# A decode kernel of two layers, its order of work and its transfers planned anew: 83 half tiles kept in place of 80

## The chip, the cores and the metric

One core of a Trainium2 chip runs the whole program in one launch. The metric is device microseconds, the time of one execution; for the kernel before it is the median of three. A profile of one more execution shows the engines: TensorE (PE, with its weight loads as PEld), VectorE (DVE), ScalarE (ACT), GpSimd (POOL), and SyncE (SP), whose queue issues nearly all transfers from main memory (HBM) into the on-chip memory (SBUF).

## The reference

Four sequences (the batch, b = 0..3) decode one token each. Twice in a row, with the same weights and the same caches both times, x goes through attention and through a gated feed-forward block:

```python
x = x + _A_ref(_layernorm(x), A_k_cache, A_v_cache, A_wq, A_wo)
x = x + _B_ref(_layernorm(x), B_w_gate, B_w_up, B_w_down)
x = x + _A_ref(_layernorm(x), A_k_cache, A_v_cache, A_wq, A_wo)
x = x + _B_ref(_layernorm(x), B_w_gate, B_w_up, B_w_down)
```

Attention has 32 query heads over 8 cached key and value heads, 4096 positions and 128 numbers a head: `softmax(q k^T / sqrt(128)) v`, then the product with wo (4096 x 512). The feed-forward block is `(sigmoid(x w_gate) * (x w_up)) w_down` with 1792 hidden columns. All data are bf16. The caches are 67 MB, so they don't fit into SBUF. Both layers read the same caches; what is still in SBUF when layer 1 asks for it needn't be read again.

## The kernel before

**Tiles and slots.** One head of one sequence has 1 MB of K and 1 MB of V; each is cut into two half tiles of 512 KB (128 partitions by 4 KB). SBUF has a ring of 28 slots (`SLOTS`), one half tile each. The string `LOADS` lists in order what SP fetches: `wq0`, `wo1`, `wu`, `wg`, `wd` are weights, and a word like `V010.` plus a character is one or two pieces of V for sequence 0, head group 1, layer 0. The characters 0 to 3 stand for a half of each of two heads, a to d for both halves of one head in one transfer of 1 MB (two slots side by side), e to h for the first and i to l for the second half of one head alone. In the text below, V010.2q1 is the second half of V of the third head of unit 010, and V010.2 is both halves.

**Units.** The work of one sequence, head group (4 of the 8 K/V heads) and layer is a unit; `UNITS` gives the 16 units in order: 000 010 011 100 001 110 200 111 210 101 211 300 310 201 311 301. A unit of layer 0 needs all its 16 half tiles loaded. A unit of layer 1 loads the half tiles that `LOADS` names for it; all others are *kept*: they stay in their slot from the layer-0 unit until then. Counted from the words of `LOADS`, the kernel before keeps 80 of 128 half tiles and loads 176 in all.

**One unit.** `unit_scores` turns each freshly loaded K tile in place on VectorE (L896) and multiplies it with the queries (L904). `GROUPS` has a digit for every unit: 4, 2 or 1 heads whose products run side by side on TensorE, each head on its own strip of 32 output rows; `HEADS` says whether a pair's two heads run together in the V products. `unit_probs` takes the softmax (L928 to L979) and `unit_values` multiplies with V (L1003), merges (L1056) and scales (L1078, L1082). Then the product with wo follows (L1108 for layer 0, L1349 for layer 1). A slot is free for a new load when the last user of its tile is done.

**The chain of a sequence.** After both head groups of a sequence's layer 0, `chain` runs its feed-forward block: gate and up products (L1217), tanh (L1249), gating (L1258), turning (L1268), the product with w_down (L1288), then mean and variance (L1330, L1197) and the next layer's queries (L826 to L855). `CUTS` says in which chunks of its 14 column blocks the middle runs; `LAST_CUTS` says the same for the last block, which handles all four sequences at once. Each chain borrows the slot of one half tile as scratch (`LENT`, one word for each chain: kind, unit, head, half). `zq` (L869) is the layout in which the queries enter the scores.

**What sets the order.** Nothing is decided on the chip. `_Plan.schedule` runs when the program is built: it goes through a model of the five engines and the transfers, with a cost for each operation, and picks on every engine the next ready operation by its rank. Ranks come from where a transfer stands in `LOADS`, plus a shift per stage (`SHIFTS`) and `CHAIN`, `PROJECT`, `KEPT_K`, `KEPT_V`, `REST_V`, `PUT_OFF`; `PATIENCE` weighs waiting for a better ranked operation. The outcome is a fixed list of instructions for each engine, with semaphore waits (L427). It also fixes which slot a load goes to, and SP issues strictly in the order of `LOADS` (L659 for K and V, L668 for weights): a load whose slot isn't free holds up all loads behind it. Where TensorE would idle, `fill_until` puts in products whose results nobody reads (L1553, 'fillers').

So a cost in the model is no cost on the chip; it only moves the order. What reaches the chip is the order, the slots, the list of loads, the groups and the cuts.

Of the kernel before, what the change touches and what calls it, by code (L numbers as in the profile page):

```python
# [17 lines left out]
DMA_LAG = 1.4  # L18
DMA_SPREAD = 0.2
DMA_START = 1.9  # L20
PATIENCE = 6.201
# [20 lines left out]
SHIFTS = {'c0': 81.66, 'c2': -0.1, 'd1': -11.9, 'd2': -26.55, 'd3': 76.83, 'm0': 8.0, 's': 77.55, 'z0': -0.3, 'z16': 4.38, 'z8': 30.04, 'z12': 50.86, 'q0': -15.2, 'v0.1': 92.64, 'o0.1': -4.74, 'w0.1': 248.14, 'k1.0': 4.46, 'p1': 45.85, 'k2.0': -9.73, 'k2.1': -29.77, 'v2.0': -5.96, 'o2.1': -101.79, 'd0': 5.31, 'q3': 51.38, 'k3.1': -52.81, 'p3': 23.58, 'v3.1': -25.26, 'k4.0': -0.08, 'k4.1': 17.87, 'p4': 24.28, 'v4.1': -24.56, 'k5.0': 19.47, 'k5.1': 3.74, 'p5': -17.71, 'v5.0': -8.59, 'v5.1': 34.03, 'w5.1': -6.54, 'p6': -80.04, 'o6.0': -17.29, 'w6.1': -3.83, 'k7.1': 8.14, 'v7.1': -5.26, 'o7.1': -29.48, 'k8.0': -34.2, 'k8.1': 17.95, 'p8': 6.04, 'v8.0': 9.7, 'o8.0': -79.15, 'v8.1': -48.83, 'p9': -1.07, 'v9.1': -42.81, 'o9.1': 15.12, 'w9.1': 1.54, 'k10.1': 20.55, 'v10.0': -41.15, 'o10.0': 9.85, 'w10.0': 36.93, 'w10.1': -3.91, 'k11.0': 7.83, 'k11.1': 36.1, 'v11.0': -4.55, 'v11.1': -2.06, 'k12.1': 314.91, 'v12.0': -16.87, 'o12.0': 1.68, 'w12.0': -0.97, 'q13': 19.97, 'k13.0': 8.85, 'k13.1': -1.52, 'p13': 139.58, 'o13.0': 113.53, 'o13.1': 4.81, 'q14': 42.47, 'k14.1': 1.8, 'p14': -41.58, 'v14.1': 15.08, 'o14.1': 8.19, 'k15.0': 1.08, 'p15': 22.58, 'v15.1': -5.53, 'o15.1': 8.17, 'end': 93.62, 'm1': -11.57, 'k9.0': 3.6, 'w9.0': -21.96, 'k14.0': -6.21, 'c1': 140.82, 'k1.1': 22.57, 'g0': 4.64, 'p2': 0.84, 'o3.1': 18.77, 'v6.0': 2.8, 'v6.1': 0.53, 'q7': -42.76, 'v7.0': 20.84, 'v9.0': -119.56, 'n2': 30.1, 'w11.1': 12.47, 'v13.0': -0.64, 'm3': -25.74, 'v14.0': -1.05, 'k0.1': -45.97, 'p0': 102.93, 'q1': 2.86, 'v1.0': -18.16, 'w3.1': -27.61, 'q5': 12.61, 'w5.0': 9.87, 'g1': -13.65, 'k7.0': 3.96, 'q8': -81.66, 'w8.0': -3.75, 'w8.1': -1.25, 'k9.1': 0.11, 'm2': -13.04, 'q10': -18.43, 'p11': -11.23, 'w11.0': -1.15, 'w12.1': 6.19, 'k0.0': 68.44, 'q2': 66.34, 'v2.1': -36.47, 'v4.0': -8.75, 'o5.0': 32.07, 'o6.1': -88.15, 'h2': 12.76, 'k10.0': -23.93, 'o10.1': -2.79, 'o11.0': -25.41, 'o12.1': 30.81, 'h3': 13.66, 'q15': 3.29, 'o15.0': 2.09, 'z24': -1.06, 'o0.0': -6.06, 'o1.0': 5.71, 'w1.0': 9.25, 'v3.0': -6.6, 'o3.0': -26.33, 'o4.0': -29.01, 'k6.0': 37.29, 'o8.1': -47.34, 'k12.0': 6.65, 'p12': 57.66, 'v12.1': -18.06, 'w0.0': -12.21, 'v1.1': 68.17, 'o1.1': 38.85, 'n0': 10.09, 'h0': 9.25, 'o5.1': -51.91, 'k6.1': 42.17, 'h1': -4.92, 'p7': 48.17, 'o7.0': -24.25, 'o9.0': -10.3, 'g2': 1.73, 'p10': -2.59, 'q11': -13.05, 'v13.1': 117.04, 'g3': 39.19, 'o14.0': -0.78, 'v15.0': 19.07}  # L42
# [392 lines left out]
def bass_interleave_layers__gqa_block_cached__glu_gated_glu__decode_kernel(nc, A_x, A_k, A_v, A_wq, A_wo, B_x, B_wg, B_wu, B_wd, out):  # L435
# [278 lines left out]
    def rank_v(u, pr):  # L714
# [19 lines left out]
        reads=["ones"] + [f"xsum{b}" for b in range(B)], writes=["U", "Uz"], cost=0.35, pairs=2,  # L734
    )
    less_b = U_ps[:, 0:4].unsqueeze(2).broadcast_to([P, B, KD])
    for o, key in ((xT, "xT"), (xc, "xc")):
# [8 lines left out]
        reads=["ones"] + [f"xsq{b}" for b in range(B)], writes=["U"], cost=0.35, pairs=2,  # L746
# [51 lines left out]
    def queries(i, rank):  # L798
# [6 lines left out]
        else:  # L805
# [16 lines left out]
            else:  # L822
# [773 lines left out]
```

## Time and profile before

| | |
|---|---|
| median of 3 runs | 285.12 us (284.92 to 286.09) |
| the profiled execution, its own time | 282.97 us |
| its span, first to last instruction | 281.1 us |
| read from HBM | 106.17 MB, 378 GB/s over the span |
| busy share of the span | PE 77%, PEld 40%, DVE 62%, ACT 23%, POOL 4% |
| transfer queue of SP | 94.3% of the time of the 16 DMA engines |

The page gives the span in 40 slices, with the busy share of each engine and the GB/s that were moved. It follows the chain that ended last back from the last instruction, and lists groups of equal instructions with their mean time. Other views list who waited for whom, or give any stretch of time with its busy times and its GB/s.

### The profile page before, as it was taken

The numbers are of one execution on the slowest core, as the hardware profiler recorded it, in microseconds if no ns is written. First come the engines' busy times: TensorE is split into PE (matmuls) and PEld (weight loads), VectorE is DVE, ScalarE is ACT, GpSimd is POOL, SyncE is SP. The second block draws the span as 40 slices with busy tenths as digits, with TensorE's granted clock in tenths as the row PEclk, the third lists the DMA queues.
The fourth block names the chain that finished last, engine by engine and source line by source line (L and its number), as shares of the span: only waits on it lengthen the run. The fifth ranks groups of instructions, "written<-read, shape, count | busy, mean of one in ns | idle before, by whom it ended". The sixth has DMA issues, their size and how long they took to land.

```text
span 281.1 us, 8157 instructions
## 1 busy us (share of the span) xinstructions
PE 217.4 (77%) x3572; PEld 112.2 (40%) x3612; DVE 174.0 (62%) x387; ACT 63.5 (23%) x155; POOL 10.7 (4%) x40
## 2 busy tenths in 40 slices
PE   1000786988889688999889886898889789989796
PEld 1000444444543343434355441355424454544464
DVE  4036379747268897858623788635999517975222
ACT  1000100052122105002132240332132312233611
POOL 5200000000000000000000000000000000000000
PEclk9999997999999999999999997999999999999999
DMA  7999999999998999999999999999999999989910
GB/s 266 429 422 426 385 417 417 411 380 397 420 369 322 417 385 427 415 416 418 420 412 387 354 419 423 415 413 422 419 417 419 423 408 366 349 293 404 421 61 3
DMA packets 21538, 106.69 MB, mean 380 GB/s; under 512 B 2048, under 2 KB 4096, under 8 KB 13056
## 3 DMA queue, kind: packets, MB, share of 16 engines
q1 hardware_dynamic: 21440, 106.18, 94.3%
q8 instruction: 28, 0.46, 0.7%
q14 instruction: 6, 0.05, 0.0%
q10 hardware_dynamic: 64, 0.01, 0.0%
HBM read 106.17 MB, written 0.00 MB: 378 GB/s over the span
## 4 chain that ended last, share of the span: by engine, by line
DMA 50%; PE 27%; DVE 10%; SPq 7%; issue 3%; ACT 1%; POOL 0%; ACTq 0%; DVEq 0%
DMA slots<-in_A_k_cache_dram 27%; DMA slots<-in_A_v_cache_dram 17%; PE S_ps L904 8%; DMA wd<-in_B_w_down_dram 7%; DVE slots L896 7%; SPq L659 4%; PE O_ps L1003 4%; PE G_ps L1288 2%; PE PT_ps L1553 2%; SPq L668 2%; PE G_ps L1553 2%; PE Q_ps L826 2%; PE M_ps L1056 1%; PE G_ps L1217 1%; PE M_ps L1349 1%
## 5 line engine op out<-in xcount | busy, mean ns | idle before, releaser
L896 DVE STREAM_TRANSPOSE slots<-slots 128x1024 int32<-128x1024 int32 x84 | 100.6, 1222 | 24.8 <-DMA slots<-in_A_k_cache_dram 24.0
L904 PE MATMUL S_ps<-slots,zq 128*32 128x512 bf16 x512 | 62.0, 401 | 7.5 <-DVE slots L896 5.3
L1003 PE MATMUL O_ps<-slots,pt_sb 128*16 128x512 bf16 x504 | 35.9, 380 | 6.2 <-DMA slots<-in_A_v_cache_dram 4.0
L1553 PE MATMUL PT_ps<-wq 128*128 128x512 bf16 (+1 forms) x123 | 33.8, 378 | 2.9 <-issue 2.7
L904 PEld LDWEIGHTS S_ps<-slots,zq 128*32 128x32 bf16 x512 | 19.7, 96 | 35.2 <-DVE slots L896 11.5
L1033 ACT ACTIVATE slots<-O_ps 128x512 bf16<-128x512 f32 (+1 forms) x26 | 15.5, 595 | 47.7 <-PE O_ps L1003 47.7
L760 PE MATMUL Q_ps<-small,wq 128*128 128x4 bf16 x128 | 3.6, 165 | 22.8 <-DMA wq<-in_A_wq_dram 22.8
L1553 PEld LDWEIGHTS PT_ps<-wq 128*128 128x128 bf16 x155 | 12.5, 98 | 19.7 <-issue 12.1
L1003 PEld LDWEIGHTS O_ps<-slots,pt_sb 128*16 128x16 bf16 x504 | 10.6, 87 | 18.3 <-ACT pt_sb L970 4.4
L1108 PEld LDWEIGHTS M_ps<-oT,wo 128*128 128x128 bf16 x512 | 14.7, 97 | 6.5 <-DVE oT L1082 2.9
L1108 PE MATMUL M_ps<-oT,wo 128*128 128x32 bf16 x512 | 16.0, 176 | 1.1 <-DVE oT L1082 0.7
L928 DVE TENSOR_REDUCE small<-S_ps 128x1 f32<-128x512 f32 x16 | 11.0, 687 | 8.7 <-PE S_ps L904 5.6
L970 ACT ACTIVATE pt_sb<-PT_ps 128x256 bf16<-128x256 f32 x32 | 10.5, 381 | 13.0 <-PE PT_ps L960 12.8
L1205 POOL TENSOR_TENSOR stat<-real,small 128x1 f32<-128x1 f32 x8 | 4.4, 549 | 233.1 <-ACT real L1201 233.1
L760 PEld LDWEIGHTS Q_ps<-small,wq 128*128 128x128 bf16 x128 | 3.5, 100 | 23.3 <-DMA wq<-in_A_wq_dram 22.9
L1056 PE MATMUL M_ps<-small,slots 128*64 128x4 bf16 (+2 forms) x204 | 9.7, 176 | 2.8 <-DVE oT L1082 1.3
L1056 PEld LDWEIGHTS M_ps<-small,slots 128*128 128x128 bf16 (+1 forms) x204 | 7.1, 103 | 11.4 <-issue 5.0
L1553 PE MATMUL G_ps<-wq 128*128 128x512 bf16 (+1 forms) x35 | 11.0, 435 | 0.6 <-issue 0.3
L949 ACT ACTIVATE p_sb<-S_ps,pt_sb,stat 128x512 bf16<-128x512 f32 x8 | 7.5, 935 | 16.5 <-DVE pt_sb L942 13.2
L770 ACT ACTIVATE oT<-Q_ps 128x64 bf16<-128x64 f32 x2 | 0.9, 448 | 43.5 <-PE Q_ps L760 43.5
L955 DVE STREAM_TRANSPOSE p_sb<-p_sb 128x256 int32<-128x256 int32 x16 | 7.0, 439 | 5.3 <-ACT p_sb L949 5.2
L869 DVE TENSOR_TENSOR zq<-Q_ps,real 128x256 bf16<-128x256 f32 x16 | 6.4, 400 | 6.1 <-ACT oT L770 5.5
(146 smaller groups left out, 222.9 us busy)
## 6 DMA issues: line engine op xcount, KB each, us to landing
slots<-in_A_v_cache_dram SPq DMA_DIRECT2D x32, 1024.0 KB, 11.1
slots<-in_A_k_cache_dram SPq DMA_DIRECT2D x29, 1024.0 KB, 10.9
slots<-in_A_v_cache_dram SPq DMA_DIRECT2D x28, 512.0 KB, 11.8
slots<-in_A_k_cache_dram SPq DMA_DIRECT2D x26, 512.0 KB, 7.6
wq<-in_A_wq_dram SPq DMA_DIRECT2D x2, 2048.0 KB, 18.5
wo<-in_A_wo_dram SPq DMA_DIRECT2D x4, 1024.0 KB, 22.0
wu<-in_B_w_up_dram SPq DMA_DIRECT2D x1, 1792.0 KB, 23.9
wg<-in_B_w_gate_dram SPq DMA_DIRECT2D x1, 1792.0 KB, 17.0
```

The source lines that it names most:

```text
L659: return e.dma_start(o, src)
L760: fns.append(lambda e, c=c, k=k: e.matmul(Q_ps[:, c * B:(c + 1) * B], lhsT=wq[:, k, hg * HC + c * DH:hg * HC + (c + 1) * DH], rhs=xT[:, :, k],
L896: "dve", lambda e, t=t: e.transpose(ring[t.slot].bitcast(dt.int32), ring[t.slot].bitcast(dt.int32)),
L904: fns.append(lambda e, s=s, t=t, nn=nn, q=q: e.matmul(S_ps[qi][32 * s:32 * s + 32, :], lhsT=window(qi, s * NQ + nn, q), rhs=ring[t.slot].r ...
L928: dve(lambda e: e.tensor_reduce(ml[at], bank, AX.X, ALU.max, negate=True), [f"S{qi}s{s}" for s in ss], keys("ml", ss), 0.7)
L949: lambda e: e.activation(p_sb[at].rearrange("p (t j r) -> p t r j", j=32, r=2), bank.rearrange("p (t r j) -> p t r j", r=2, j=32), ACTF.Ex ...
L970: "act", lambda e, pr=pr: e.activation(pt_sb[:, (2 * i + pr) % 3], PT_ps[:, 256 * pr:256 * pr + 256], ACTF.Copy),
L1003: fns.append(lambda e, m=m, at=at, v=v, c=c, q=q, pt=pt, bank=bank, x0=x0, x1=x1: e.matmul(bank[m:m + 16, x0:x1], lhsT=pt[:, at:at + 16], ...
L1033: lambda e, lent=lent, rows=rows, o_ps=o_ps, rows_of=rows_of, cols=cols: e.activation(ring[lent.slot][rows, 0:cols], rows_of(o_ps[rows, 0: ...
L1056: return e.matmul(o, lhsT=turned[:, tt * P + at:tt * P + at + n], rhs=heads(tt), start=(tt == 0), stop=(tt == 3))
L1108: fns.append(lambda e, k=k, n=n, h0=h0: e.matmul(M_ps[:, k * WIDE:(k + 1) * WIDE], lhsT=wo[:, h0 + n, k * P:(k + 1) * P], rhs=oT[:, b, h0 ...
L1553: return lambda e: e.matmul(ps_of[:, 0:width], lhsT=wq[:, 0, 0:P], rhs=wq[:, 0, 0:width], start=True, stop=True)
```

## The change

Some costs in the plan's model are set to other values: small f32 products 0.35 to 0.2, the tanh pieces from 0.18 + 0.47 s to 0.26 + 0.39 s and the turned pieces from 0.13 + 0.24 s to 0.16 + 0.42 s (s is the share of the 14 column blocks), `zq` 0.35 to 0.41, a few more. Transfers are modelled to land 0.3 us later (`DMA_SPREAD`) and to be held up more by instruction fetches (`DMA_LAG`). With these, all that was searched is given anew: the ranks' shifts, the groups, the cuts, the lent tiles, and the list of loads. Counted from the words of the new `LOADS`, 83 of 128 half tiles are kept and 173 are loaded; the transfers of 1 MB stay 61, those of a half tile go from 54 to 51. How many of the 28 slots hold kept half tiles behind some of the units:

| after unit | 010 | 011 | 100 | 110 | 200 | 210 | 101 | 300 | 310 | 201 | 311 |
|---|---|---|---|---|---|---|---|---|---|---|---|
| before | 23 | 9 | 15 | 21 | 21 | 22 | 16 | 6 | 20 | 20 | 6 |
| after | 24 | 9 | 15 | 21 | 21 | 22 | 16 | 8 | 22 | 22 | 8 |

The operations of a unit, the weights and the arithmetic are as before. The diff, without the shifts of the stages and with one of each kind of cost:

```diff
-DMA_LAG = 1.4
+DMA_LAG = 1.55
-DMA_SPREAD = 0.2
+DMA_SPREAD = 0.5
-PATIENCE = 6.201
+PATIENCE = 10.377
...
-CUTS = "0 4 14"
+CUTS = "0 6 14"
-LAST_CUTS = "0 6 8 14"
+LAST_CUTS = "0 6 10 14"
-GROUPS = "1441441444214244"
+GROUPS = "4141211442414144"
-HEADS = "2212222122222222"
+HEADS = "2222122222222222"
-LENT = "V00031 V20030 V10110 V21111 V20110"
+LENT = "V01031 V20020 V10101 K20100 V20110"
-CHAIN = -3108.651
+CHAIN = -2570.724
-PROJECT = 2584.665
+PROJECT = 2919.577
-KEPT_K = -953.257
+KEPT_K = -1842.097
-KEPT_V = -2637.133
+KEPT_V = -3091.275
-REST_V = 88.299
+REST_V = 253.576
...
-PUT_OFF = -380.691
+PUT_OFF = -1023.963
-LOADS = "V000a V000d V010g wq1 K010b V010b K000d K000a wq0 V010k K000b wo1 K010a K010k V000c K000c V010a K010g K010d wu V000b wo3 wo0 V010d wo2 wg wd K100g K100h V011j K011j K100l V100e K100i K001a K100e K100b K001d K100k V001f K110d V100i V100b V100d K110c K110b K110a V001d V100k K200d K200c V100g K200a K200b V110e V110i V110b V110d V110c V200c V200h V200l V2000 V2001 K210l K210k K210g K210a V111l K210h K101g K101d K210b V210b K101e V210a K300c V210d V210c V101j V101i V101d V101g V101k K300b K310a K310c K300a K300d V300a K201e K310b K310d V300c V300d V300b V310b V310a V310c V310d K201f K201h K301g K201g K201j K201i K2013 V201i V201f V201e V201j K301f V201c K301k V201d V311d V301e V301b V301c V301h V301l"
+LOADS = "V010b V010k K010a K010g wq0 K010b K010k wq1 V000a V000d K000a K000c K010d K000b K000d V000c V010d wo3 wo0 V000b V010a wo2 wu wo1 K100h V010g wg wd K100l K100f K100e K100i K100j V100f K001a K100c V100j V001j V011l K001l K001c K200c V100h K200h V100l V100c K200l K200b K110a K110b V100a K110c K110d K200a V001k V110a V110b V110c V110d V200h V200c V200l V200i V2000 V200j K210f K210l K210h K210c V111e K210j K210a K101d V210a K101b V210d V210b V210c V101b V101d V101c K300c K300a K310b K300b V300d K310d K300d K310c K310a V300a V300c V300b V310a V310b V310d V310c K201h K201l K201g K201e K201f K201k K201j V201g K201i V201h K301g V2013 V201f K301k V201j V201a V311c V301b V301k V3012 V301l"
...
-        reads=["ones"] + [f"xsum{b}" for b in range(B)], writes=["U", "Uz"], cost=0.35, pairs=2,
+        reads=["ones"] + [f"xsum{b}" for b in range(B)], writes=["U", "Uz"], cost=0.2, pairs=2,
...
-                S.put("pe", fns, reads=[own("P"), "sel"], writes=[own("Q")], cost=0.25, rank=rank, free="P")
+                S.put("pe", fns, reads=[own("P"), "sel"], writes=[own("Q")], cost=0.09, rank=rank, free="P")
...
-        S.put("pe", fns, reads=[key, "even"], writes=[own("Q", l == 0)], cost=0.25, rank=rank, lock="Q" if l == 0 else None)
+        S.put("pe", fns, reads=[key, "even"], writes=[own("Q", l == 0)], cost=-0.21, rank=rank, lock="Q" if l == 0 else None)
...
-            reads=[own("Q"), by_key], writes=[f"qz{qi}"], cost=0.35, rank=rank, free="Q",
+            reads=[own("Q"), by_key], writes=[f"qz{qi}"], cost=0.41, rank=rank, free="Q",
...
-                keys("nM", ss) + rs_key, keys("nM", ss), 0.16,
+                keys("nM", ss) + rs_key, keys("nM", ss), 0.23,
...
-            reads=keys("ls", ss) + ["sel_h"], writes=[own("M", True)], cost=0.35, rank=rank + 1.0, lock="M", pairs=2,
+            reads=keys("ls", ss) + ["sel_h"], writes=[own("M", True)], cost=0.2, rank=rank + 1.0, lock="M", pairs=2,
-        dve(lambda e: e.reciprocal(rl[:, qi, hs], M_ps[:, hs]), [own("M")], keys(f"rl{qi}", ss), 0.18, free="M")
+        dve(lambda e: e.reciprocal(rl[:, qi, hs], M_ps[:, hs]), [own("M")], keys(f"rl{qi}", ss), 0.26, free="M")
...
-                "pe", fns, reads=["sel_o"] + ([own("P")] if lent is None else ["half"] if alone else []), writes=[own("M", True)], cost=0.25, rank=late,
+                "pe", fns, reads=["sel_o"] + ([own("P")] if lent is None else ["half"] if alone else []), writes=[own("M", True)], cost=0.07 if two else 0.03, rank=late,
...
-            cost=0.18 + 0.47 * share, rank=rank,
+            cost=0.26 + 0.39 * share, rank=rank,
...
-            reads=[own("P") + f"t{c0}", own_th + "0"], writes=[own_th + f"d{c0}"], cost=0.13 + 0.24 * share, rank=rank,
+            reads=[own("P") + f"t{c0}", own_th + "0"], writes=[own_th + f"d{c0}"], cost=0.16 + 0.42 * share, rank=rank,
```

More of the change, by code (lines that the diff above doesn't have):

```diff
@@ L745, in bass_interleave_layers__gqa_block_cached__glu_gated_glu__decode_kernel @@
         "pe", lambda e: e.matmul(U_ps[:, 4:8], lhsT=ones, rhs=xsq, start=True, stop=True),
-        reads=["ones"] + [f"xsq{b}" for b in range(B)], writes=["U"], cost=0.35, pairs=2,
+        reads=["ones"] + [f"xsq{b}" for b in range(B)], writes=["U"], cost=0.2, pairs=2,
     )
@@ L1153, in mean_part @@
             "pe", lambda e: e.matmul(o, lhsT=ones, rhs=column, start=start, stop=stop),
-            reads=reads + ["ones"], writes=["U"], cost=0.1 if start and not stop else 0.35, rank=rank, pairs=2,
+            reads=reads + ["ones"], writes=["U"], cost=0.1 if start and not stop else 0.2, rank=rank, pairs=2,
         )
@@ L1197, in rstd @@
             "pe", lambda e: e.matmul(ps_tile[:, 16:17], lhsT=by, rhs=xsq[:, b:b + 1], start=True, stop=True),
-            reads=[f"xsq{b}", by_key], writes=[bank], cost=0.35, rank=rank, pairs=2, **first,
+            reads=[f"xsq{b}", by_key], writes=[bank], cost=0.2, rank=rank, pairs=2, **first,
         )
@@ L1421, in last_part @@
             "pe", lambda e: e.matmul(U_ps[:, 0:B], lhsT=ones, rhs=xsum, start=True, stop=False),
-            reads=["ones"] + [f"xsum{b}" for b in every_b], writes=["U"], cost=0.35, pairs=2, rank=rank,
+            reads=["ones"] + [f"xsum{b}" for b in every_b], writes=["U"], cost=0.2, pairs=2, rank=rank,
         )
```

8 lines of the change are left out of this document (4 added, 4 removed).

## The prediction

> **What bounds the kernel now.** I read the page first: its engines, its slices and the chain of waits.
>
> ```profile
> span 281.1 us, 8157 instructions
> ...
> PE 217.4 (77%) x3572; PEld 112.2 (40%) x3612; DVE 174.0 (62%) x387; ACT 63.5 (23%) x155; POOL 10.7 (4%) x40
> ...
> DMA  7999999999998999999999999999999999989910
> GB/s 266 429 422 426 385 417 417 411 380 397 420 369 322 417 385 427 415 416 418 420 412 387 354 419 423 415 413 422 419 417 419 423 408 366 349 293 404 421 61 3
> ...
> HBM read 106.17 MB, written 0.00 MB: 378 GB/s over the span
> ...
> DMA 50%; PE 27%; DVE 10%; SPq 7%; issue 3%; ACT 1%; POOL 0%; ACTq 0%; DVEq 0%
> ```
>
> The transfers bound it. The DMA digit is 9 from the second slice to the 38th, and half of the chain that ended last is DMA. TensorE is busy 77%, but much of that is fillers. So the time is four things: a start, the bytes at the rate of an undisturbed stretch, what is lost where the rate dips, and the work behind the last landing. Stretches of the span show the last three. The columns are the stretch, its length, busy time (and instructions) of PE, PEld, DVE, ACT and POOL, the granted clock, the DMA share and GB/s.
>
> ```profile
> 20.00:30.00 10.00, 0.46 (x17) 0.46 (x18) 4.74 (x4) 0.00 (x0) 0.00 (x0) 1.00 1.02 422
> 77.00:89.00 12.00, 10.79 (x164) 5.23 (x163) 8.54 (x18) 1.98 (x7) 0.55 (x1) 1.00 0.92 343
> 150.00:158.00 8.00, 6.66 (x153) 4.04 (x147) 4.09 (x14) 3.09 (x9) 0.61 (x2) 1.00 0.96 341
> ...
> 234.00:253.00 19.00, 17.48 (x290) 8.78 (x296) 15.75 (x38) 5.12 (x15) 1.10 (x2) 1.00 0.92 330
> 253.00:269.00 16.00, 13.95 (x289) 7.54 (x284) 6.38 (x23) 7.42 (x16) 0.00 (x0) 1.00 0.94 386
> 269.00:281.00 12.00, 9.60 (x216) 6.82 (x215) 3.70 (x18) 2.27 (x7) 0.55 (x1) 1.00 0.02 6
> ```
>
> 422 GB/s is the undisturbed rate. Against it three stretches lose time: 12 x (1 - 343/422) = 2.2 us while sequence 0's chain ends, 8 x (1 - 341/422) = 1.5 us at sequence 1's, and 19 x (1 - 330/422) = 4.1 us while unit 201 is loaded and sequence 3's chain runs. About 12 us follow the last landing.
>
> **The bytes.** The change loads 173 half tiles in place of 176; the transfers that go away are three of a half tile.
>
> ```profile
> slots<-in_A_v_cache_dram SPq DMA_DIRECT2D x28, 512.0 KB, 11.8
> slots<-in_A_k_cache_dram SPq DMA_DIRECT2D x26, 512.0 KB, 7.6
> ```
>
> These 54 become 51 (25 of K, 26 of V). 3 x 524288 B = 1.573 MB. At 422 GB/s that is 3.73 us; at the whole span's 378 GB/s it is 4.16 us. I take 3.9: half tiles are mostly loaded in the slow stretches, but a slow stretch loses its time to waits rather than to bytes. One K tile fewer is turned (DVE, off the bound), nothing else of a unit's work goes away.
>
> The Trainium skill (DMA: Bandwidth & Descriptors, Specifications) gives a core some 358 GB/s from HBM. By that 1.573 MB would be worth 4.39 us and the forecast 0.5 us lower; the trace disagrees with it, 422 GB/s over 10 us.
>
> **What the kept tiles cost: slots.** A kept half tile holds a slot. Two places with a dip get tighter by the counts of the list of loads, and these are the other two terms.
>
> *Sequence 0's chain.* Rows of the chain of waits (start, length), then of SP's waits from 77 to 90 us (total, times, longest), then of SP's own queue:
>
> ```profile
> 60.24 18.97 DMA wd<-in_B_w_down_dram
> 79.35 1.56 PE G_ps L1288 x56
> ...
> 83.70 0.58 PE S_ps L904 x4
> 84.28 0.22 PE Q_ps L855 x13
> ```
>
> ```profile
> SPq L427 <- PE G_ps L1288: 13.2, 1, 13.2
> SPq L427 <- PE Q_ps L855: 3.2, 1, 3.2
> ```
>
> ```profile
> 66.40 14.91 SPq L659 DMA_DIRECT2D slots<-in_A_k_cache_dram  x2
> 84.54 0.33 SPq L659 DMA_DIRECT2D slots<-in_A_v_cache_dram  x1
> ```
>
> wd lands at 79.3, the product with it ends at 80.9, unit 011's queries are there at 84.5. Until then SP stands: 13.2 us for the chain's scratch slot, then 3.2 us. What keeps the DMA engines busy meanwhile is what is queued behind wd. Before, 23 slots are kept and one is lent, so 4 half tiles (K100.2q0, K100.3q0, V011.1q1, K011.1q1) stand behind wd: 2.10 MB, 5.0 us at 422 GB/s, and the dip starts about that long after wd. After, 24 are kept and one is lent, so 3 are free, and K100.3q0 goes ahead of wd: 2 half tiles behind it, 2.5 us, while wd itself lands 1.24 us later (one half tile ahead of it). Bounds: two half tiles of cover lost is 2.5 us at most. The other end is 0: unit 100 is of layer 0, doesn't need this chain, and its scores do run before unit 011's (the S_ps row at 83.70 stands ahead of the queries' row at 84.28), and the new list puts the unkept K100.3 and K100.1 first, whose slots come back after their scores. I take +1.0, nearer to the lower end, since such slots return during the 16 us of waiting. Chunks of 6 and 8 in place of 4 and 10 in the chain are costed at nothing: the chain's tanh rows move by 0.05 us (372 to 421 ns for the first chunk), hidden under the wait for wd in this chain and under transfers in the others.
>
> ```profile
> L1249 ACT ACTIVATE slots<-G_ps,stat 128x128 f32<-128x128 f32 x4 | 1.5, 372 | 2.9 <-POOL stat L1205 2.9
> L1249 ACT ACTIVATE slots<-G_ps,stat 128x192 f32<-128x192 f32 x2 | 0.8, 421 | 1.7 <-POOL stat L1486 1.7
> ```
>
> *Unit 201.* SP's waits from 222 to 253 us, two stretches of 2 us, the fillers (L1553) in the stretch, and scores (L904): 16 products of four heads side by side, then 4 products of one head alone.
>
> ```profile
> SPq L427 <- PE S_ps L904: 7.8, 3, 2.7
> SPq L659 <- PE O_ps L1003: 7.3, 1, 7.3
> ```
>
> ```profile
> 248.00:250.00 2.00, 2.00 (x40) 0.88 (x36) 0.67 (x4) 0.99 (x2) 0.00 (x0) 1.00 1.04 287
> 250.00:252.00 2.00, 1.84 (x32) 0.84 (x25) 1.90 (x7) 0.65 (x2) 0.00 (x0) 1.00 0.59 246
> ```
>
> ```profile
> 234.00:253.00 19.00, 2.38 (x8) 0.84 (x12) 1.00 0.92 330
> ```
>
> ```profile
> 122.12 1.04 PE L904 MATMUL S_ps<-slots,zq 128*32 128x512 bf16 x16
> ...
> 126.39 1.04 PE L904 MATMUL S_ps<-slots,zq 128*32 128x512 bf16 x4
> ```
>
> Here slots circulate: a load, a turn, a score, and SP may load again; it waited 7.8 us for scores. Before, 20 are kept and V211's lent tile holds one until the chain ends: 7 circulate. After, 22 are kept and the lent tile is K201.0q0, held from its load on: 5 or 6. Against that, unit 201's scores run head by head (`GROUPS` 2 to 1), so a slot comes back without waiting for its neighbour; but a group costs 1.04 us whether it has one head or four, so 8 groups in place of 4 cost TensorE 4 x 1.04 = 4.2 us, where its fillers are 2.38 us and its idle time 19 - 17.48 = 1.5 us: cover of 3.9 us, just short. Unit 301 has two half tiles fewer to load around here, which are already in the bytes. Bounds: if the earlier return wins, half of today's 4.1 us goes (-2). If the stage runs throughout at the mean of its two worst stretches, 267 GB/s, its 19 x 0.330 = 6.27 MB take 23.5 us: +4.5. I take +0.6: the counts pull upward, the finer groups back.
>
> The Trainium skill (DMA: Bandwidth & Descriptors, Anatomy of one DMA) gives every transfer about 2.0 us beside its bytes, from setup to completion. That speaks against fewer slots: a half tile issued into an empty queue would cost 3.2 us in place of 1.2, and two such restarts would make this term +4.0 and the sum -3.9 + 1.0 + 4.0 = +1.1: 286.2 us, between the last two rivals below. No row shows a restart by itself; the median half tile lands 7.6 us after its issue, mostly queue.
>
> **The rest.** Over all units `GROUPS` gives 72 groups of scores in place of 60: 12 x 1.04 = 12.5 us more on TensorE, under fillers elsewhere; they take 44.8 us after 20 us of the span:
>
> ```profile
> 20.00:281.00 261.00, 44.82 (x158) 16.45 (x198) 0.99 0.95 380
> ```
>
> If that cover failed in one unit of layer 0, it would cost up to 4.2 us there. The dip at sequence 1's chain has as many kept slots as before (21): 0, between -1.5 and +1.0. The tail has the same four last half tiles' work; the last chunks 6, 4, 4 in place of 6, 2, 6 feed this row,
>
> ```profile
> 276.95 1.49 PE G_ps L1288 x56
> ```
>
> 56 products that TensorE runs without a gap: 0, within 0.3 us. The start loads other tiles first at the same rate and reads both halves of wq earlier: 0. Costs in the plan alone run nowhere.
>
> **The sum.** -3.9 + 1.0 + 0.6 = -2.3 us. On the profiled execution that is 281.1 - 2.3 = 278.8 us of span, 282.97 - 2.3 = 280.7 us of its own time (1.87 us lie around the span). The median of the runs stands 2.15 us above the profiled execution, so the forecast for it is 282.8 us.
>
> **The rivals.**
>
> *The bytes in full.* The finer groups and the new order keep the dips as they are or better: 285.1 - 3.9 = 281.2, and 279.7 if sequence 1's dip (1.5 us) goes as well. For it: SP's long waits are for a few late events, which an order can move. Against it: fewer slots at the two worst places.
>
> *The stalls take all of it.* Sequence 0's chain costs its full 2.5 and unit 201 about 1.4 more: 285.1. For it: SP is strictly in order, and both dips are waits for slots. Against it: unit 011 now has all its K kept, so its scores wait for no load.
>
> *Slower: unit 201 runs short of slots and of TensorE together.* With 5 slots circulating and 4.2 us more scores against 3.9 us of cover, the stage falls to 267 GB/s: 285.1 - 3.9 + 1.0 + 4.5 = 286.7. It decides from the point where the stage loses 4.3 us more than today (3.9 - 1.0 + 1.4). For it: TensorE is at 17.48 of 19 us there. Against it: two half tiles of unit 301 don't have to come through.
>
> *The order alone.* All ranks are new, so any stage may be better or worse; this has no sign of its own and is in the width.
>
> **How the numbers follow.** About 0.5%, 1.4 us, is what a measurement of this kernel can tell from no change. The forecast, 281.9 to 283.7, has a chance of 0.38; the bytes in full 0.22; the stalls take all 0.24; slower 0.16. Faster by over 0.5% (below 283.7) is the first two: 0.60; within 0.5% 0.24; slower 0.16. The range runs from 280.2 (into the first rival's better end, 279.7) to 286.6 (up to the slower rival, 286.7).
>
> **What would show it.** In the profile after: 51 half tiles and 104.6 MB read; a dip around 77 to 89 us longer by about a us, with SP waiting for L1288; 330 GB/s or less around unit 201, with SP waiting for L904 and few fillers there; 12 us behind the last landing. I am wrong if the dips shrink (then the list of loads and not the slots set them), if TensorE sets unit 201's stage, or if the tail moves by more than 0.5 us.

## The result, and the profile after

In 18 runs of each kernel side by side the kernel before took 285.21 us (median; 283.66 to 286.46) and the kernel after 286.60 us (285.77 to 289.35). The ratio is 1.0053, with an interval of 1.0032 to 1.0074: **slower by 1.5 us** (0.9 to 2.1; the medians stand 1.4 apart). The forecast was 282.8 us and faster. Medians are over all runs of a kernel, while ratios leave out the slow ones, those over 1.5% above the fastest of the same kernel (375.75 us is the extreme here).

Two executions of the kernel after were profiled, of 289.35 and 284.38 us. The second stands 1.41 us above the profiled execution of before (282.97), as the medians stand 1.39 apart, so it is the one that is read here. Both profiled executions that are compared lie below all 18 runs of their kernel, so the sizes read from them are those of two quick executions. Lines of its page, in the order of the lines shown of before:

```profile
span 282.3 us, 8360 instructions
...
PE 243.5 (86%) x3694; PEld 122.3 (43%) x3694; DVE 172.7 (61%) x386; ACT 63.7 (23%) x155; POOL 10.7 (4%) x40
...
DMA  7999999999977999999999999999999999699910
GB/s 270 427 418 424 419 419 385 408 395 383 421 302 230 374 420 414 417 423 417 418 415 382 337 423 425 417 419 420 421 416 424 419 409 348 230 324 407 416 59 3
...
HBM read 104.60 MB, written 0.00 MB: 371 GB/s over the span
...
PE 58%; DMA 31%; DVE 5%; SPq 4%; issue 1%; ACT 1%; DVEq 0%; ACTq 0%
...
slots<-in_A_v_cache_dram SPq DMA_DIRECT2D x26, 512.0 KB, 11.0
slots<-in_A_k_cache_dram SPq DMA_DIRECT2D x25, 512.0 KB, 8.3
```

The bytes went down as forecast (104.60 MB, 51 half tiles), and yet the span is 1.2 us longer. The DMA digit, 9 through nearly all of before, now has two holes: slices 12 and 13, at 78 to 92 us (302 and 230 GB/s), and slice 35. In slices 34 to 36, at 233 to 254 us, 366, 349 and 293 GB/s have become 348, 230 and 324. The chain that ended last is now 58% TensorE, where it was 27%.

To put sizes to that, stretches of the span from 80 us on (up to there both kernels move 397 GB/s); columns as in the prediction. Kernel before:

```profile
80.00:110.00 30.00, 25.52 (x359) 11.51 (x359) 25.30 (x45) 7.15 (x19) 0.55 (x1) 1.00 0.97 379
110.00:150.00 40.00, 36.09 (x487) 17.48 (x489) 23.81 (x50) 8.37 (x21) 0.48 (x1) 1.00 1.02 416
150.00:170.00 20.00, 16.48 (x346) 8.91 (x337) 14.91 (x32) 6.42 (x16) 0.61 (x2) 1.00 1.00 387
170.00:230.00 60.00, 51.34 (x852) 25.41 (x861) 41.26 (x95) 16.19 (x39) 1.10 (x2) 0.97 1.01 417
230.00:269.70 39.70, 35.65 (x633) 18.35 (x638) 23.77 (x66) 13.47 (x31) 1.10 (x2) 1.00 0.92 354
269.70:281.10 11.40, 8.89 (x192) 6.17 (x193) 3.70 (x18) 1.94 (x6) 0.55 (x1) 1.00 0.01 3
```

Kernel after:

```profile
80.00:110.00 30.00, 29.68 (x363) 12.66 (x358) 21.39 (x40) 7.18 (x19) 0.55 (x1) 1.00 0.88 337
110.00:150.00 40.00, 34.94 (x473) 16.36 (x473) 28.45 (x59) 8.82 (x21) 0.00 (x0) 1.00 1.02 418
150.00:170.00 20.00, 18.82 (x371) 9.64 (x367) 12.26 (x32) 6.08 (x16) 1.10 (x2) 1.00 0.98 380
170.00:230.00 60.00, 59.14 (x884) 28.20 (x877) 42.89 (x95) 16.80 (x40) 1.10 (x2) 1.00 1.01 420
230.00:270.50 40.50, 39.09 (x662) 20.74 (x663) 24.15 (x68) 13.33 (x31) 1.10 (x2) 1.00 0.89 339
270.50:282.30 11.80, 9.69 (x213) 6.75 (x209) 3.61 (x18) 2.01 (x7) 0.55 (x1) 0.97 0.01 3
```

A stretch loses its length times (1 - its rate / 422), with 422 GB/s as the undisturbed rate. Behind 269.7 and 270.5 us next to nothing is moved, so these rows are the tails.

| stretch | loss before, us | loss after, us | difference, us |
|---|---|---|---|
| 0 to 80 | 4.7 | 4.7 | 0 |
| 80 to 110, sequence 0's chain | 30 x (1 - 379/422) = 3.1 | 30 x (1 - 337/422) = 6.0 | +3.0 |
| 110 to 150 | 0.6 | 0.4 | -0.2 |
| 150 to 170, sequence 1's chain | 1.7 | 2.0 | +0.3 |
| 170 to 230 | 0.7 | 0.3 | -0.4 |
| 230 to the last landing | 39.7 x (1 - 354/422) = 6.4 | 40.5 x (1 - 339/422) = 8.0 | +1.6 |
| behind the last landing | 11.4 long | 11.8 long | +0.4 |
| bytes, 1.573 MB at 422 GB/s | | | -3.7 |

The sum is +1.0 us; the spans differ by +1.2. The bytes bring what they should, and two dips give it back with more: twice as much at sequence 0's chain as at unit 201.

**Sequence 0's chain.** TensorE's instructions from 78 to 92 us (start, length), the product with wd and the first full run of unit 011's scores. Kernel before:

```profile
79.35 1.55 PE L1288 MATMUL G_ps<-slots,wd 128*128 128x32 bf16 x56 [0.86 <-DMA wd<-in_B_w_down_dram]
...
84.57 2.85 PE L904 MATMUL S_ps<-slots,zq 128*32 128x512 bf16 x34
```

Kernel after, with the fillers ahead of that product:

```profile
80.27 1.47 PE L1553 MATMUL PT_ps<-wq 128*128 128x512 bf16 x6
81.57 1.55 PE L1288 MATMUL G_ps<-slots,wd 128*128 128x32 bf16 x56
...
85.43 0.82 PE L904 MATMUL S_ps<-slots,zq 128*32 128x512 bf16 x3
...
88.28 1.99 PE L904 MATMUL S_ps<-slots,zq 128*32 128x512 bf16 x32 [0.20 <-DVE zq L869]
```

The product with wd starts 2.2 us later, with fillers up to it in place of a wait for wd. Only 1.3 us of that are wd's: it lands at 80.5 us (issued at 63.70, landed 16.8 us later) in place of 79.2. The rest is the middle of the chain, whose last turned piece is ready at 81.8 us in place of 78.8. Between the product and unit 011's scores another 1.5 us are lost (6.7 us in place of 5.2), with scores of unit 100 in between (they run ahead of 88.28 us, where the wait for unit 011's queries, zq, ends). So the scores come **3.7 us later**. SP's queue in the kernel after from 79 us on, and its waits from 77 to 90 us:

```profile
80.41 0.33 SPq L659 DMA_DIRECT2D slots<-in_A_k_cache_dram  x1
83.22 0.33 SPq L659 DMA_DIRECT2D slots<-in_A_k_cache_dram  x1
86.33 0.33 SPq L659 DMA_DIRECT2D slots<-in_A_k_cache_dram  x1
88.00 0.33 SPq L659 DMA_DIRECT2D slots<-in_A_v_cache_dram  x1
89.41 1.25 SPq L659 DMA_DIRECT2D slots<-in_A_k_cache_dram  x2
```

```profile
SPq L427 <- PE S_ps L904: 17.9, 3, 13.9
SPq L427 <- PE G_ps L1288: 2.4, 1, 2.4
```

Two half tiles stand behind wd (issued at 65.40 and 66.09 us), as the prediction counted. After them SP waits 13.9 us for the scores of one half tile of unit 100 (K100.3q0), whose fourth product TensorE takes only at 79.95 us, behind the chain's gate and up products. Then slots come back one at a time: at 83.22 the chain's scratch slot, at 86.33 and 88.00 by scores of unit 100. Loads come close together from 89.41 us on; before, from 85.24 us.

**Unit 201.** SP's waits from 222 to 253 us in the kernel after, and TensorE's and its fillers' time in the prediction's stretch:

```profile
SPq L427 <- PE S_ps L904: 10.1, 7, 3.1
SPq L659 <- PE O_ps L1003: 8.3, 1, 8.3
```

```profile
234.00:253.00 19.00, 18.88 (x263) 9.53 (x259) 15.43 (x36) 4.04 (x12) 1.10 (x2) 1.00 0.84 296
```

```profile
234.00:253.00 19.00, 2.25 (x7) 0.70 (x7) 1.00 0.84 296
```

SP waits seven times for scores in place of three, 10.1 us in place of 7.8; the stretch moves 296 GB/s in place of 330. TensorE is full, but 2.25 us of it are still fillers.

### The profile page after: what moved, and what is told of

It is laid out like the page before. It is cut to its first block, busy times and chain, and to the rows that moved or that the text cites. A ratio compares the mean times of both kernels' runs of the same rounds, so it can differ in the third digit from the quotient of the medians.

```text
span 287.4 us, 8318 instructions
## 1 busy us (share of the span) xinstructions
PE 240.9 (84%) x3652; PEld 123.1 (43%) x3694; DVE 173.2 (60%) x386; ACT 63.7 (22%) x155; POOL 10.7 (4%) x40
## 3 DMA queue, kind: packets, MB, share of 16 engines
q1 hardware_dynamic: 21008, 104.60, 91.6%
HBM read 104.60 MB, written 0.00 MB: 364 GB/s over the span
## 4 chain that ended last, share of the span: by engine, by line
PE 53%; DMA 33%; DVE 6%; SPq 4%; issue 3%; ACT 1%; ACTq 0%; DVEq 0%
DMA slots<-in_A_k_cache_dram 21%; PE S_ps L904 13%; DMA slots<-in_A_v_cache_dram 12%; PE PT_ps L1553 11%; PE O_ps L1003 7%; DVE slots L896 4%; PE G_ps L1553 3%; SPq L659 3%; PE M_ps L1108 3%; PE M_ps L1056 2%; PE G_ps L1288 2%; PE Q_ps L783 1%; PE G_ps L1217 1%; PE PT_ps L960 1%; PE Q_ps L826 1%
## 5 line engine op out<-in xcount | busy, mean ns | idle before, releaser
L896 DVE STREAM_TRANSPOSE slots<-slots 128x1024 int32<-128x1024 int32 x83 | 99.5, 1224 | 21.9 <-DMA slots<-in_A_k_cache_dram 21.1
L904 PE MATMUL S_ps<-slots,zq 128*32 128x512 bf16 x512 | 73.8, 399 | 4.1 <-DVE slots L896 2.4
L1553 PE MATMUL PT_ps<-wq 128*128 128x512 bf16 (+1 forms) x183 | 48.7, 376 | 3.5 <-issue 2.9
L1003 PE MATMUL O_ps<-slots,pt_sb 128*16 128x512 bf16 x504 | 39.2, 388 | 4.3 <-DMA slots<-in_A_v_cache_dram 3.9
L904 PEld LDWEIGHTS S_ps<-slots,zq 128*32 128x32 bf16 x512 | 23.4, 96 | 35.5 <-DVE slots L896 9.2
L1553 PEld LDWEIGHTS PT_ps<-wq 128*128 128x128 bf16 x217 | 18.2, 101 | 24.8 <-issue 12.5
L1553 PE MATMUL G_ps<-wq 128*128 128x512 bf16 (+1 forms) x55 | 14.9, 376 | 1.0 <-issue 0.7
L949 ACT ACTIVATE p_sb<-S_ps,pt_sb 128x512 bf16<-128x512 f32 x8 | 6.7, 838 | 30.4 <-DVE pt_sb L942 29.2
L1082 DVE TENSOR_TENSOR oT<-M_ps,real 64x8 bf16<-64x8 f32 x32 | 5.2, 162 | 12.0 <-PE M_ps L1056 11.7
L835 ACT ACTIVATE p_sb<-Q_ps 128x512 bf16<-128x512 f32 x8 | 4.8, 597 | 25.8 <-PE Q_ps L826 24.6
```

What stands on the lines that cost most here:

```text
L896: "dve", lambda e, t=t: e.transpose(ring[t.slot].bitcast(dt.int32), ring[t.slot].bitcast(dt.int32)),
L904: fns.append(lambda e, s=s, t=t, nn=nn, q=q: e.matmul(S_ps[qi][32 * s:32 * s + 32, :], lhsT=window(qi, s * NQ + nn, q), rhs=ring[t.slot].r ...
L949: lambda e: e.activation(p_sb[at].rearrange("p (t j r) -> p t r j", j=32, r=2), bank.rearrange("p (t r j) -> p t r j", r=2, j=32), ACTF.Ex ...
L1003: fns.append(lambda e, m=m, at=at, v=v, c=c, q=q, pt=pt, bank=bank, x0=x0, x1=x1: e.matmul(bank[m:m + 16, x0:x1], lhsT=pt[:, at:at + 16], ...
L1553: return lambda e: e.matmul(ps_of[:, 0:width], lhsT=wq[:, 0, 0:P], rhs=wq[:, 0, 0:width], start=True, stop=True)
```

## The experiments

In the kernels called **held**, each compute engine takes its operations in the order of the kernel they come from; only slots, transfers and fillers are planned anew for the edit. That is done by recorded lists and this in the planner:

```diff
                 for op in queue[e]:
+                    if e in held_order and op.key in known[e] and op.key != held_order[e][0]:
+                        continue
```

Each ratio is to runs of the kernel before on the same chip.

**The kernel after once more**, with no edit:

> The kernel after, unchanged, profiled once more, since the profile at hand is the slowest of its 18 executions (289.35 us against a median of 286.6 us; granted clock 0.976). Slots theory: the dip at sequence 0's chain and the one around unit 201 are there again, at about 7 us and 6 us lost against 422 GB/s, because they come from the order of loads and the kept slots. Rival, late TensorE: the half-clock window at 40 to 46 us made TensorE late and its fixed fillers kept it late; without that window there the first dip shrinks by 2 us or more and sequence 0's product with wd starts before 81 us in place of 83.1 us.

284.38 us; its stretches are those above. Both dips are there again, so they belong to the kernel. The rival has a part: in the execution of 289.35 us, with more time at half clock (last section), the product with wd starts at 83.12 us and the stretch from 80 to 110 us loses 7.7 us; here it is 81.57 and 6.0, so 1.6 us of that dip went with the execution.

**Two slots more, in the kernel after and in the kernel before.** All are held. w_up gets no place of its own: it is loaded into w_gate's place, w_gate is loaded over it, and both products take w_gate, so these kernels leave the product with w_up out. The control has the same with 28 slots.

```diff
-    wu = sb("wu", [P, KD, F], bf)
+    wu = wg
...
-    SLOTS = 28
+    SLOTS = 30
```

> Control for the next run: the kernel after with the order of its compute engines held as it is; w_up has no place of its own but is loaded into w_gate's place, ahead of w_gate, so the up product multiplies with w_gate in place of w_up (this part of the computation is changed; its work and its bytes are not). 28 slots as before the change. Both theories: the time of the kernel after, 286.6 us within 0.5 us, since w_gate only has to wait for w_up, which lands some us earlier than w_gate's turn.

> As the control, with 30 slots in place of 28 (the room that w_up leaves); same bytes, same held order on the compute engines, up product with w_gate's columns. Slots theory: the loads stop waiting, the two dips lose some 3 to 4 us less together, and the time is 2.5 to 3.5 us below the control. Late TensorE: the dips come from TensorE being late and not from slots; within 1 us of the control.

> The kernel before with the order of its compute engines held, w_up loaded into w_gate's place (the up product takes w_gate, so the numbers are not the reference's), and the space given to two more slots: 30. It is the counterpart of the 30 slots in the kernel after, which gained 5.0 us there (286.83 to 281.83). Theory A, the three further kept tiles have made slots the limit that they weren't before: here 30 slots gain 1 us at most against the kernel before, ratio 0.996 to 1.003. Theory B, slots bind both kernels alike, and the change only moved along the same limit: a gain of 3 to 5 us, ratio 0.982 to 0.99.

The control gives 286.83 us, ratio 1.0061 (1.0013 to 1.0110): that holding the order or w_up's place changes the kernel after is not seen. With 30 slots it takes 281.83 us, 0.9900 (0.9865 to 0.9935), 5.0 us less by the medians and 4.6 by the ratios. The kernel before with 30 slots, for which the one control has to do, takes 280.46 us, 0.9834 (0.9801 to 0.9868), 4.7 us less by the ratio. So two slots are worth some 4.6 to 5.0 us, 2.3 to 2.5 for one on average, **in either kernel**: about twice a half tile's 1.24 us of bytes, and the view that the three kept tiles first made slots the limit falls: they were it before. The kernel before with 30 slots, from 80 to 110 us:

```profile
80.00:110.00 30.00, 26.46 (x379) 12.08 (x378) 25.65 (x47) 8.16 (x21) 0.55 (x1) 1.00 1.00 403
```

That is a loss of 1.4 us in place of 3.1. In the kernel after, the same stretch with 30 slots stays a dip; below it unit 201's stretch, which moved 296 GB/s with 28:

```profile
80.00:110.00 30.00, 29.71 (x378) 13.11 (x372) 21.27 (x40) 7.45 (x20) 1.10 (x2) 1.00 0.85 331
```

```profile
234.00:253.00 19.00, 18.89 (x275) 9.51 (x274) 15.67 (x39) 4.70 (x15) 1.10 (x2) 1.00 0.98 363
```

The two slots don't help at sequence 0's chain. Its first six loads behind wd are out by 84.23 us in place of 88.00, but the seventh, K001.0, is a transfer of 1 MB that needs two slots side by side, and it goes out at 90.44 us, when unit 011's scores (from 89.31 us) give them back. So here it is the time at which TensorE's order gives slots back that sets the dip, not their count. Around unit 201 they do help: 363 GB/s with TensorE as full as before and SP waiting for scores just as often (7 times, 10.2 us). So neither TensorE nor the finer groups hold that stretch at 296; two more loads in the queue make the difference. From 150 to 170 us the rate goes from 380 to 414 GB/s as well.

**A half tile ahead of wd, in the kernel before** (held), which is the change's own move done alone:

```diff
-... V010d wo2 wg wd K100g K100h ...
+... V010d wo2 K100g wg wd K100h ...
```

> The kernel before, order of the compute engines held; K100.2q0 goes ahead of w_gate and w_down in place of behind w_down, as a half tile does in the kernel after. Late-chain theory: w_down lands 1.24 us later and so the whole chain, and there is one half tile less behind it: 2 to 2.7 us slower than before. The step of the prediction (a half tile of cover and of delay costs about 1.0 us, since unit 100's slots come back meanwhile): 0.7 to 1.3 us slower. Nothing, if the dip has no part in the time: within 0.5 us.

286.51 us, ratio 1.0078 (1.0049 to 1.0108): +2.2 us (1.4 to 3.1). The prediction's +1.0 lies below the interval. TensorE's rows, and the stretch from 80 to 110 us:

```profile
80.63 1.55 PE L1315 MATMUL G_ps<-slots,wd 128*128 128x32 bf16 x56
...
85.85 2.87 PE L931 MATMUL S_ps<-slots,zq 128*32 128x512 bf16 x34
```

```profile
80.00:110.00 30.00, 25.28 (x348) 11.87 (x351) 24.20 (x45) 6.03 (x16) 0.55 (x1) 1.00 0.92 357
```

The product with wd and unit 011's scores both move by 1.28 us (lines are 27 further down in this kernel), a half tile's time, and the stretch loses 30 x (1 - 357/422) = 4.6 us in place of 3.1. So here the half tile ahead of wd costs 1.5 us, little more than the delay. Another 1.3 us are lost from 150 to 170 us (360 GB/s in place of 387), far from the edit; why is open. The price of 2.2 us is thus that of the whole plan with this edit, and the part at the chain, 1.5 us, is near the lower end of its interval.

**w_up behind the K and V tiles, in the kernel after** (held): if the chain was late because V010.2q0 and wo1 land late, loading them 4.3 us earlier should help.

```diff
-... wo2 wu wo1 K100h V010g wg wd ...
+... wo2 wo1 K100h V010g wu wg wd ...
```

> The kernel after, order of the compute engines held; in the list of loads w_up is moved from before wo1 and K100.3q0 to behind V010.2q0, so wo1 and unit 010's last V tile land 4.4 us earlier, while w_gate and w_down stay where they are. Late-chain theory (the dip at sequence 0's chain is long because the chain's middle waits for wo1 and V010.2q0, and unit 011's scores, which give back the kept slots, come 3 to 4 us later than before the change): the product with wd starts 0.5 to 2.5 us earlier (81.6 to 83.1 us so far), the dip loses 1 to 2 us less, the time is 1 to 2 us below the kernel after, about 285 us. Slots theory (cover behind wd alone): wd lands as late as it did, nothing changes, 286.6 us within 0.5 us.

287.08 us, ratio 1.0078 (1.0043 to 1.0114): no gain over the kernel after. The product with wd starts at 81.94 us:

```profile
74.41 3.40 PE L1580 MATMUL PT_ps<-wq 128*128 128x512 bf16 x15 [0.16 <-issue]
...
81.94 1.55 PE L1315 MATMUL G_ps<-slots,wd 128*128 128x32 bf16 x56
```

An earlier V010.2q0 and wo1 bring nothing here. wd lands at 80.4 us, as it did, and the product starts 1.5 us behind it: the upper row is a run of fillers up to the gate product at 77.75 us, although w_gate landed at 76.1 us (issued at 58.97, landed 17.1 us later). In this kernel, then, fillers hold up the middle of the chain, and what the earlier tiles would bring without them the run doesn't show.

**No fillers before 75 us, in the kernel after** (held): do the fillers, which are planned up to a landing that the model puts late, hold up the chain?

```diff
-FILL_FROM = 30.0
+FILL_FROM = 75.0
```

> The kernel after, order of the compute engines held, without the fillers on TensorE before 75 us of the plan (about 90 fewer; products whose results nobody reads). Late-TensorE theory: real work starts when its data is there and not behind fillers, so the product with wd starts 1 to 2 us earlier and the time falls by 1 to 2 us, unless the granted clock falls to half in that stretch. Slots and late-chain theories: the fillers are no cause by themselves; with the clock at half between 60 and 80 us the chain is later and the time 1 to 4 us longer, else unchanged.

286.72 us, ratio 1.0085 (1.0055 to 1.0116): no gain. The product with wd comes 0.9 us earlier, just behind wd (80.6 us), and unit 011's scores 1.1 us earlier (87.18 us). But without fillers the granted clock is halved for long:

```profile
80.68 0.75 PE L1315 MATMUL G_ps<-slots,wd 128*128 128x32 bf16 x24 [0.33 <-DVE p_sb L1285]
```

```profile
53.00:63.00 10.00, 8.01 (x118) 3.69 (x112) 4.70 (x12) 2.81 (x7) 0.00 (x0) 0.50 1.02 401
```

So fillers make this chain about a us late, but that us isn't what the dip costs: the stretch from 80 to 110 us moves 337 GB/s, as with them, where the slots that come back one at a time do so 0.4 to 0.8 us earlier (loads at 79.68, 82.54, 85.53 and 87.64 us). Whether the fillers cost the kernel after anything at full clock, and what those behind 75 us cost, this run can't tell.

**One more kept tile, in the kernel before** (held): V301.0q0 stays from unit 300 on, 81 kept, 175 loaded.

```diff
-... V311d V301e V301b ...
+... V311d V301b ...
```

> The kernel before, order of the compute engines held, one more half tile kept: V301.0q0 isn't loaded again (175 loads in place of 176, 81 kept), so one slot more is taken from unit 300 to unit 301. Slots theory: the bytes (1.24 us at 422 GB/s) are more than paid back around unit 201; 0 to 1.5 us slower than before. Bytes in full: 1.0 to 1.3 us faster than before.

287.71 us, ratio 1.0103 (1.0067 to 1.0138): **+2.9 us for a load less**. The interval is 1.9 to 3.9. With 1.24 us of bytes saved, the slot it takes away costs 4.2 us. V301.0q0 is one of the three tiles that the change keeps in addition. The stretch from 230 to 262 us in the kernel before, and with the tile kept, a loss of 7.4 us in place of 4.6:

```profile
230.00:262.00 32.00, 28.62 (x494) 14.08 (x495) 22.03 (x58) 9.54 (x24) 1.10 (x2) 1.00 0.96 362
```

```profile
230.00:262.00 32.00, 27.15 (x443) 13.54 (x450) 20.20 (x50) 7.96 (x21) 1.10 (x2) 1.00 0.91 325
```

**K301.1 loaded again, in the kernel after** (held): 81 kept, 175 loaded, and two slots more circulate behind unit 300. Only the first of these halves is kept newly by the change; the kernel before keeps the second one too.

```diff
-... K201f K201k K201j ... K301k V201j ...
+... K201f K301f K201k K201j ... K301j K301k V201j ...
```

> The kernel after with two half tiles no longer kept: both halves of K of unit 301's second head are loaded again (175 loads of a half tile in place of 173, 81 kept); order of the compute engines held, two turns of K tiles on VectorE added. Slots theory: what the two half tiles cost in bytes (2.5 us at 422 GB/s) comes back as a shorter dip around unit 201; the time stays within 0.8 us of the kernel after. Rival, bytes count in full and the dip has another cause: 2.0 to 3.0 us slower than the kernel after (about 289 us).

> The kernel after with its order held, which loads both halves of K301.1 again in place of keeping them: 81 kept as one more than before, 1.05 MB more. The earlier look at it is to be settled. Theory A, the bytes count in full: 2.0 to 3.0 us above the kernel after, ratio to the kernel before 1.012 to 1.016. Theory B, the two slots are worth their bytes: within 0.8 us of the kernel after, 1.003 to 1.008. Theory C, from the kernel before with one slot more kept (4 us for a slot against 1.24 us of bytes): 2 us or more below the kernel after, 0.998 at most.

Four runs gave 288.29 us, 1.0137 (1.0096 to 1.0177); twelve on another chip 287.39 us, 1.0086 (1.0054 to 1.0118). Against the kernel after's 1.0053 that is +2.4 us and +0.9 us, together about +1.5 us with 0.9 either way. Keeping these two tiles thus brings something, but on these runs less than their 2.5 us of bytes: some 1.0 us (0.1 to 1.9) goes for their slots. The interval of the sum ends just below 2.5, so this is the weakest of the readings. The traces go with it: from 234 to 253 us the two profiled executions move 375 and 363 GB/s, where the kernel after moves 296. That keeping them was a loss (theory C) is excluded.

**Unit 201 head by head, in the kernel before** (held):

```diff
-GROUPS = "1441441444214244"
+GROUPS = "1441441444214144"
```

> The kernel before with its order held, and unit 201's scores in eight groups of one head in place of four groups of two, as after; nothing else. The prediction: 4 x 1.04 = 4.2 us more on TensorE against 3.9 us of cover, so +0.3 us, within 0.8 of the kernel before. Theory A, the finer groups are what unit 201's stage lost: +1.2 to +2.5 us. Theory B, slots that come back head by head are worth more than TensorE's time: -0.5 to -2 us.

285.72 us, ratio 1.0017 (0.9989 to 1.0044): +0.5 us, between -0.3 and +1.3. The +0.3 of the prediction's working, 4.2 us of products against 3.9 us of cover, lies in that interval; that finer groups speed the slots up is not seen. The profiled execution (286.81 us) is no pattern for the stretch: its clock was halved in the midst of it, and the rate fell to 223 GB/s there:

```profile
237.60:241.00 3.40, 3.40 (x37) 1.44 (x33) 2.76 (x5) 0.45 (x2) 0.55 (x1) 0.54 0.65 223
```

**The planner's costs alone**: the kernel after with all that was searched as before (ranks' shifts, groups, cuts, lent tiles, list of loads), nothing held.

> The first half of the change alone: the planner's new durations and landing times with all that was searched as before (order shifts, groups, cuts, lent tiles, list of loads). The 176 loads and their order are the same; only the order on the compute engines, the slots and the fillers are planned anew. Theory A, an order that was searched for one set of durations isn't good for another: +3 to +8 us. Theory B, the list of loads sets the time and the order within the engines little: within 1.5 us of the kernel before.

291.87 us, ratio 1.0252 (1.0209 to 1.0295): +7.2 us with the same 106.17 MB. Its fillers from 20 to 281 us take 71.8 us, which were 44.82 us before. Its stretches:

```profile
80.00:110.00 30.00, 28.02 (x360) 12.39 (x361) 23.81 (x43) 6.04 (x16) 0.55 (x1) 1.00 0.93 364
150.00:170.00 20.00, 17.47 (x344) 9.31 (x349) 11.54 (x28) 6.08 (x16) 1.10 (x2) 1.00 0.96 349
230.00:278.90 48.90, 46.55 (x751) 24.80 (x754) 24.82 (x71) 14.44 (x33) 1.10 (x2) 1.00 0.84 321
```

These lose 4.1, 3.5 and 11.7 us (the third runs to the last landing), where the kernel before loses 3.1, 1.7 and 6.4. The durations alone undo the order that was searched for others; the new search wins back 1.0252 - 1.0053 = 0.0199, 5.7 us, and ends 1.5 us short of where the old costs and the old search were.

## Why the prediction was wrong, point by point

- **Bytes, -3.9: right.** 51 half tiles and 104.60 MB; 3.7 us at the undisturbed rate. But it set the tiles' bytes against slots in two places only. The runs show that a slot has a price, and that it depends on where and in which order it is held: 2.3 to 2.5 us for one throughout the span, 4.2 us for the one in V301.0q0 in the kernel before, about 1.0 us for the two of K301.1 in the kernel after.
- **Sequence 0's chain, +1.0: this step failed.** It measured +3.0, beyond its upper bound of 2.5. Its counts were right (two half tiles behind wd, wd one half tile later). What was wrong was to halve the lost cover by slots that "return during the 16 us of waiting". They hardly did: the first of unit 100's slots came back after 13.9 us, at 80.41 us, the next two at 86.33 and 88.00 us. And the step had no term for the end of the chain, whose scores free the slots: they come 3.7 us later, 1.3 us by wd's landing, 0.9 us by the middle of the chain and the fillers, and 1.5 us as scores of unit 100 are put between the chain's products. The half tile ahead of wd alone, in the kernel before, costs 2.2 us in all and 1.5 us in this stretch. That the place of unit 100's scores in TensorE's order makes the rest is read from the trace; no run changes it alone. The chunks' tanh and turning, which the prediction hid under the wait for wd, are no longer hidden in this chain: wd is there 1.3 us before the last turned piece.
- **Unit 201, +0.6: sign right, size +1.6** for all from 230 us on. The finer groups by themselves are +0.5 us (-0.3 to +1.3). The rest goes with the slots: in the kernel after with 30 slots, and with K301.1 loaded again, the stretch moves 363 to 375 GB/s in place of 296, and holding one slot more in the kernel before hits the same stretch. How much the new order adds wasn't separated.
- **Chunks, fillers, sequence 1's chain, tail at 0: nearly right**, +0.3 and +0.4 us. The extra scores of the finer groups are hidden by that, as said. But the fillers didn't shrink with them: they take 72.8 us in place of 44.8, which the prediction had no term for.
- **The offset to the median** (2.15 us above the profiled execution): 285.21 - 282.97 = 2.24 in the new runs, and 286.60 - 284.38 = 2.22 after. The second is no test, as this execution was taken for standing where it does; the other one lies 2.75 us above the median.
- **The rivals.** Nearest by its mechanism was "the stalls take all of it" (285.1, with 2.5 and 1.4 us where 3.0 and 1.6 were measured). The slower rival's 286.7 is within 0.1 us of the result, but that is luck: it put the loss into unit 201 at 267 GB/s, and the larger part is at sequence 0's chain. No slower rival had its place there. The range's upper end of 286.6 is just the median.

In the kernel after, loads that go out alone take longer than their bytes: of those that SP issued from 77 to 105 us, the fastest landed 3.6 us after its issue, and the four issued from 80.41 to 88.00 us took 3.6 to 4.4 us, of which a half tile's bytes are 1.24 us. The Trainium skill (DMA: Bandwidth & Descriptors, Anatomy of one DMA), weighed in the prediction with two restarts and 286.2 us, gives some 2.0 us beside the bytes, for transfers that GpSimd issues; these are SP's, and their 2.4 us and more are near it.

```profile
DMA to landing us min/median/max: 3.6/11.0/15.5
```

The prediction looked for such restarts at unit 201; here they stand at sequence 0's chain. It also said that no row shows one, but the kernel before has one, issued at 84.54 us and landed after 3.3 us. How much of the dip they make wasn't measured.

A reckoning from the runs of single parts doesn't close: -3.7 us for the bytes, +2.2 for the half tile ahead of wd and +0.5 for the groups leave the slots. With the 4.2 us that V301.0q0's slot costs in the kernel before, the sum is +3.2 us; with the 1.0 us for the two of K301.1 in the kernel after, it is 0.0; measured is +1.5 (0.9 to 2.1). Each of these parts has an interval of about a us either way, and the price of a slot differs between the two orders, so the parts can't simply be added. The slot of the third tile (in unit 011), the place of unit 100's scores, the lent tiles, the heads and the added fillers behind 75 us weren't tried alone. Nor was K100.3q0 put behind wd in the kernel after, because the order of its engines has that tile's turn ahead of the chain's gating, and a plan without that is another order throughout.

## What to carry to other kernels

Price a kept tile by the slot it holds, not only by the bytes it saves: with 28 slots, two more were worth about twice their bytes in either kernel, and one tile more kept made the kernel before 2.9 us slower. A transfer that goes ahead of a weight which a serial chain waits for costs its own time at least where that chain's end releases the slots (here 2.2 us, 1.4 to 3.1, for 1.24 us of bytes). Before counting on slots that come back during such a wait, look where the work that frees them stands in the fixed order. New costs in a planner, however good, are a new problem for the search: compare the stage rates of the two outcomes before taking the new one.

## What the runs showed of the hardware

TensorE's granted clock drops to half for stretches of 3.4 us or a multiple of it (10 us in the kernel without fillers before 75 us), at different places in different executions of one kernel. In the kernel after, once:

```profile
37.00:40.00 3.00, 0.12 (x4) 0.13 (x5) 2.88 (x5) 0.15 (x1) 0.00 (x0) 0.88 1.02 423
39.30:42.70 3.40, 2.83 (x52) 1.92 (x53) 3.40 (x5) 0.30 (x1) 0.00 (x0) 0.50 0.99 414
```

TensorE was busy 0.12 us of the three before 40 us and 0.81 us of the 3.4 before 39.3. This goes with what the Trainium skill states (TensorE: Matmul & The Clock Gate, Part 1: The HAM clock gate): an idle window of about 3.4 us halves the clock, and the windows run freely and don't restart with the kernel. In the execution of 289.35 us it was halved in three places, at 39.3 us for 6.8 us, and at 148.5 and 169.0 us for 3.4 us each. Here the 3.4 us ahead of 148.5, those at half clock, and the stretch that follows:

```profile
145.10:148.50 3.40, 3.03 (x67) 2.11 (x66) 1.51 (x8) 1.96 (x6) 0.00 (x0) 1.00 1.02 419
148.50:151.90 3.40, 2.96 (x24) 0.95 (x26) 0.26 (x2) 0.67 (x2) 0.00 (x0) 0.50 1.01 406
150.00:170.00 20.00, 17.34 (x364) 10.31 (x362) 9.81 (x33) 5.59 (x15) 1.10 (x2) 0.93 0.92 331
```

TensorE was busy 3.03 of the 3.4 us before this one, so by these rows an idle window is not what halved the clock there. From 150 to 170 us this execution moves 331 GB/s, the other one 380 at full clock: 2.3 us more are lost. I take the half clock for a part of the 3 to 4 us by which executions of one kernel differ; no run here isolates it.
